# Zero products at the start, a table built in six parts and transposes moved forward, in a convolution and spectral-mixing kernel on one core

## The chip, the core and the metric

The kernel runs on one core of one Trainium2 chip. The core has five engines that run their own instruction streams and meet through semaphores: TensorE (PE in the profile; its weight loads are listed apart as PEld), VectorE (DVE), ScalarE (ACT), GpSimd (POOL) and SyncE (SP). Transfers between the chip's main memory and the on-chip memory are issued by POOL and SP and carried out by 16 DMA engines. The time that counts is the device time of one execution in microseconds (us).

## The reference

Two operators stand one behind the other. The input `x` has 8 batches of 3264 positions with 192 channels.

The first is a causal convolution over the positions with 7 taps, one set of taps for each of 8 heads of 24 channels; the taps go through a softmax first. The second mixes in the frequency domain:

```python
X = np.fft.rfft(x, axis=1)                       # x: the convolution's result
Xr, Xi = np.real(X[:, :64]), np.imag(X[:, :64])  # the 64 lowest modes
Yr = einsum('bmd,mde->bme', Xr, w_r) - einsum('bmd,mde->bme', Xi, w_i)
Yi = einsum('bmd,mde->bme', Xr, w_i) + einsum('bmd,mde->bme', Xi, w_r)
y = np.fft.irfft(Y, n=3264, axis=1)              # all other modes are zero
u = x + y
out = u + np.maximum(u @ w_ch, 0.0)
```

So 20 MB of float32 come in as `x`, 19 MB as the mode weights `w_r` and `w_i` (64 matrices of 192 x 192 each), and 20 MB go out.

## The kernel before

**Tiles.** The batches are taken in four pairs (`q`), and the 3264 positions of a pair in tiles of 128; a last half tile of 64 is shared out over the pairs. A pair has six units of 5, 5, 4, 4, 4 and 4 tiles, so there are 24 units (`UNITS`, `units`). All of `x` stays on chip as bfloat16 in `xall`; the conversion is done by the transfers. The convolution's result is written back into `xall`, one slot further down.

**Start.** POOL issues the loads of `x` for all units in order, with some index tables (`iota`), the identity `ident` and the signed permutation `perm` made between them, and behind them the first half of the mode weights. The loads of `x` wait for no engine's work, only for a free place among eight transfers in flight. SP loads the taps. DVE and ACT make the softmax and spread the taps into a banded matrix, `band`, which the convolution multiplies by on PE.

**The table.** `ftab` holds cosines and sines for the forward transform, 27 rows of 128 columns. `table(t0, t1)` makes its rows `t0` to `t1`: three operations on DVE (product of position and mode, rounding to whole turns, subtraction) and three on ACT (Sin, Abs, Sin). `PARTS` cuts it in three: 5, 9 and 13 rows. The first part stands ahead of the loop over the units, the second and third behind the convolution's copies of the first two units. The temporaries `kprod` and `turns` lie in `arena`, where the mode weights go later.

**The loop over units.** For unit `k`: `conv` (32 to 48 products on PE into the two PSUM tiles `Z`; then one copy back to `xall` on ACT, line 342, and one on DVE, line 344), then for a finished pair `xtrans` of one batch (the transform's result is transposed by products with `ident` and `perm`, and copied into `xt`, which shares its space with the later `zw` under the name `mixa`, on DVE, line 369), then `dft_unit` of the unit before (products of 128 x 384 with the table, line 350, summed over a pair in PSUM), then in two of three units `some(1)`: one job of the list `tjobs`, here `c_bank`, eight transposes of `xall` into `cc` (line 405). Transposed banks are copied by `copy`, which takes ACT for every third and DVE for the others:

```python
    def copy(out, in_):
        ncopy[0] += 1
        if ncopy[0] % 3 == 0:
            nc.scalar.copy(out=out, in_=in_)
        else:
            nc.vector.tensor_copy(out=out, in_=in_)
```

**From the loop to the mixing.** Behind the loop come the last `dft_unit`, whose result ACT copies to `xs` (line 357), the issue of eight groups of weights, `xtrans` of the last two batches, and the jobs `g_bank` (transposes of the table itself, line 394; 104 products in eight banks, the first four banks with 52 of them for one half of it), which are put at the head of `tjobs`.

**Mixing.** Sixteen groups of four modes. `mix(g)` multiplies a group (line 457, 12 products). Four weight groups lie in `arena`, four in the part of `cc` that is not yet used. Groups 8 to 11 are loaded once `mix(0)` to `mix(3)` have freed their places, groups 12 to 15 once `mix(8)` to `mix(11)` have (POOL, line 446). Between the `mix` calls stand jobs of `tjobs`, a number for each group by the list `PLAN`, and products with `w_ch` made ahead (`c_ahead`, line 521).

**Last stage.** For each block of output: products with `w_ch` (line 531) and the inverse transform (line 551) on PE, the maximum on ACT (line 613), the addition on DVE (line 638), the store from POOL or SP (lines 646 and 651).

All orders are written out by hand: an engine runs its instructions in the order of the program's text.

Of the kernel before, what the change touches and what calls it, by code (L numbers as in the profile page):

```python
# [10 lines left out]
ACT = mybir.ActivationFunctionType  # L11
# [8 lines left out]
def kernel(  # L20
# [9 lines left out]
    nc = tc.nc  # L30
    B, S, D = x.shape
# [5 lines left out]
    P = 128  # L37
    NQ = B // 2
    NF = S // P
    NT = NF + 1  # L40
# [5 lines left out]
    MAGIC = 12582912.0  # L46
    UNITS = ((0, 5), (5, 5), (10, 4), (14, 4), (18, 4), (22, 4))
    units = [(q, t0, n) for q in range(NQ) for t0, n in UNITS]
    PARTS = ((0, 5), (5, 14), (14, NF + 2))

    pool = ctx.enter_context(tc.tile_pool(name="main", bufs=1))

    def sb(name, shape, dtype, **kw):
        return pool.tile([P] + shape, dtype, tag=name, name=name, **kw)
# [36 lines left out]
    halfpi = sb("halfpi", [1], F32)  # L91
    xs = [sb(f"xs{i}", [2, D], BF16) for i in range(2)]
# [26 lines left out]
    def temp(n, dtype):  # L119
        w = n * 2 if dtype in (F32, mybir.dt.int32) else n  # L120
        a = arena[:, pos[0]:pos[0] + w]
        pos[0] += (w + 15) // 16 * 16
        return a.bitcast(dtype) if dtype != BF16 else a
# [3 lines left out]
    turns = temp(NTM * MODES, F32)  # L127
# [19 lines left out]
    def psum_pool(name, side):  # L147
        stack = ExitStack()
        return stack, stack.enter_context(tc.tile_pool(name=name, bufs=1, space=PSUM, side=side))
# [4 lines left out]
    low = [pp.tile([P, 512], F32, tag=f"low{i}", name=f"low{i}") for i in range(4)]  # L154

    def slot(q, t):
        return NT * q + t

    def load_unit(q, t0, n, only=None):
        nf = min(n, NF - t0)  # L160
        s0 = slot(q, t0) + 1
        for i in range(2) if only is None else (only,):
# [17 lines left out]
                   allow_small_or_imprecise_dtypes=True)  # L180
    nc.gpsimd.iota(midx, pattern=[[1, MODES]], base=0, channel_multiplier=0,
                   allow_small_or_imprecise_dtypes=True)
    nc.vector.memset(halfpi[:], math.pi / 2)
    nc.vector.memset(packed, 0.0)
    for a in (band[:].rearrange("p h c -> p (h c)"), xall[:, NT:NSLOT:NT, 1, :]):
# [6 lines left out]
    nc.vector.tensor_tensor(out=wsub.rearrange("p (h k) -> p h k", h=H), in0=wr3,  # L192
                            in1=wmax.unsqueeze(2).to_broadcast([P, H, KK]), op=ALU.subtract)
    nc.scalar.activation(out=wexp, in_=wsub, func=ACT.Exp)
    we3 = wexp.rearrange("p (h k) -> p h k", h=H)
    nc.vector.reduce_sum(out=wsum, in_=we3, axis=AX.X)
    nc.vector.tensor_scalar(out=wsum, in0=wsum, scalar1=1e-9, scalar2=None, op0=ALU.add)
# [15 lines left out]
    kp3 = kprod.rearrange("p (t m) -> p t m", t=NTM)  # L213
    tu3 = turns.rearrange("p (t m) -> p t m", t=NTM)

    def table(t0, t1):
        sh = [P, t1 - t0, MODES]
        kp, tu = kp3[:, t0:t1, :], tu3[:, t0:t1, :]
        nc.vector.scalar_tensor_tensor(out=kp, in0=sidx[:, t0:t1].unsqueeze(2).to_broadcast(sh), scalar=1.0 / S,
                                       in1=midx.unsqueeze(1).to_broadcast(sh), op0=ALU.mult, op1=ALU.mult)  # L220
        nc.vector.tensor_scalar(out=tu, in0=kp, scalar1=MAGIC, scalar2=-MAGIC, op0=ALU.add, op1=ALU.add)
        nc.vector.tensor_tensor(out=kp, in0=kp, in1=tu, op=ALU.subtract)
        nc.scalar.activation(out=ftab4[:, t0:t1, :, 1, :], in_=kp.rearrange("p t (h m) -> p t h m", h=2),
                             func=ACT.Sin, scale=-TWOPI)
        nc.scalar.activation(out=tu, in_=kp, func=ACT.Abs)
        nc.scalar.activation(out=ftab4[:, t0:t1, :, 0, :], in_=tu.rearrange("p t (h m) -> p t h m", h=2),
                             func=ACT.Sin, scale=-TWOPI, bias=halfpi[:, 0:1])
        if t1 > NF:
            nc.vector.memset(ftab[HALF:P, NF, :], 0.0)
            nc.vector.memset(ftab[0:HALF, NF + 1, :], 0.0)  # L230

    table(*PARTS[0])
    def load_half(g, i):
        src = bass.AP(tensor=x.tensor, offset=x.offset + ((4 * g + i) * S + P * NF) * D,
                      ap=[[D, HALF], [2 * S * D, 2], [1, D]])
        nc.gpsimd.dma_start(out=xall[HALF * (i ^ g):HALF * (i ^ g) + HALF,  # L236
                                     NT * (2 * g + 1):NT * (2 * g + 2) + 1:NT, 0, :], in_=src)
# [93 lines left out]
    def conv(q, t0, n):  # L331
        done = [conv_step(q, t0, n, half, 0) for half in range(2)]
        for half in range(2):
            turn(done[half])
            conv_step(q, t0, n, half, 1)
        s0 = slot(q, t0)
        for half in range(2):
            cp = Z[half][:, :, :].rearrange("p k (j c) -> p (k j) c", j=2)
            dst = xall[:, s0:s0 + n, :, 96 * half:96 * half + 96].rearrange("p t i (j e) -> p j (t i) e", j=4)
            srcv = cp[:, :, 0:2 * GRP * n].rearrange("p j (c e) -> p j c e", e=GRP)  # L340
            if half == 0:
                nc.scalar.copy(out=dst, in_=srcv)  # L342
            else:
                nc.vector.tensor_copy(out=dst, in_=srcv)  # L344

    def dft_unit(q, t0, n):
        xp = low[0][:, 0:2 * D]
        for t in range(t0, t0 + n):
            if t < NF:
                nc.tensor.matmul(xp, ftab[:, t, :], xall[:, slot(q, t), :, :], start=(t == 0), stop=False,  # L350
                                 skip_group_check=True)
            else:
                for i in range(2):
                    nc.tensor.matmul(xp[:, D * i:D * i + D], ftab[:, NF + (i ^ q // 2), :], xall[:, slot(q, t), 0, :],
                                     start=False, stop=(i == 1), skip_group_check=True)
        if t0 + n == NT:
            nc.scalar.copy(out=xs[q % 2][:], in_=xp.rearrange("p (i d) -> p i d", i=2))

    def xtrans(q, i, bank):
        tp = low[1 + bank][:, 0:3 * P].rearrange("p (j c) -> p j c", j=3)  # L360
        xsv = xs[q % 2][:, i, :].rearrange("k (p j) -> k j p", j=3)
        for j in range(3):
            nc.tensor.matmul(tp[0:64, j, :], xsv[:, j, :], ident[:], start=True, stop=True,
                             tile_position=(0, 0), skip_group_check=True)
            nc.tensor.matmul(tp[64:P, j, :], xsv[:, j, :], perm[:], start=True, stop=True,
                             tile_position=(0, 64), skip_group_check=True)
        b = 2 * q + i
        for h in range(2):
            nc.vector.tensor_copy(out=xt[:, h, :, b:2 * B:B, :],
                                  in_=tp[:, :, 64 * h:64 * h + 64].rearrange("p j (c m) -> p j c m", c=2))  # L370
# [42 lines left out]
    tjobs = []  # L413
# [3 lines left out]
    def some(n, upto=NT * NQ):  # L417
        for _ in range(n):
            if tjobs and tjobs[0][0] < upto:
                _, f, *a = tjobs.pop(0)  # L420
                f(*a)
# [2 lines left out]
    waiting = []  # L424
    for k, u in enumerate(units):
        conv(*u)
        if k < 2:
            table(*PARTS[k + 1])
        if waiting:
            xtrans(*waiting.pop(0), 0)  # L430
        if k:
            q, t0, n = units[k - 1]
            dft_unit(q, t0, n)
            if t0 + n == NT:
                waiting = [(q, 0), (q, 1)]
            if k > 1:
                some(XJOBS[k], min(NT * q + t0 + n, NT * (NQ - 1)))
    dft_unit(*units[-1])


    NG = MODES // 4
# [42 lines left out]
    conv_stack.close()  # L484
    ring_stack, pp = psum_pool("pring", "left")
    ring[:] = [pp.tile([P, 512], F32, tag=f"r{i}", name=f"r{i}") for i in range(4)]
    xtrans(NQ - 1, 0, 0)
    xtrans(NQ - 1, 1, 1)
    tjobs = [(0, g_bank, c, t0, min(8, NT - t0)) for c in (1, 0) for t0 in range(0, NT, 8)] + tjobs

# [219 lines left out]
    for n in range(N + 1):  # L712
# [5 lines left out]
        elif given(n + 2):  # L718
            nc.scalar.copy(out=items[n + 2][1][:, :, 0:2 * D].rearrange("p k (a d) -> p k a d", a=2),
                           in_=halves.rearrange("p (k a) d -> p k a d", k=2))  # L720
# [39 lines left out]
```

## Time and profile before

| what | value |
|---|---|
| time, median of 4 runs (lowest to highest) | 177.32 us (176.48 to 177.88) |
| time of the profiled execution | 176.88 us |
| its span, first to last instruction | 174.7 us |
| busy time: PE, PEld | 149.0 us (85%), 109.1 us (62%) |
| busy time: DVE, ACT, POOL | 119.4 us (68%), 105.6 us (60%), 100.6 us (58%) |
| transfers | 40.17 MB as written on chip or sent out, mean 230 GB/s |
| main memory read, written | 39.40 MB, 20.05 MB |
| first product on PE | 10.54 us |
| first product of the first `mix` | 73.89 us |
| first product of the last `mix` | 107.45 us |

The span is what the profile shows; the profiled execution's own time is 2.2 us longer. In the rows of slices each digit is the busy share of 1/40 of the span in tenths. A line of the timeline gives start and length in us, the engine, the source line, the operation, what it writes and reads, and in brackets how long the engine had been idle and what ended that. PE products overlap each other, so the length over a group is not the sum of its products. GB/s counts the bytes at their on-chip size, so the loads, which convert from float32 to bfloat16, read twice that from main memory.

### The profile page before, as it was taken

To read this page: it belongs to the slowest core of one execution; us is meant where nothing else is said; L and a number is where in the kernel's file an instruction comes from. 1 tells how busy PE (TensorE), PEld (TensorE's weight loads), DVE (VectorE), ACT (ScalarE), POOL (GpSimd) and SP (SyncE) were. 2 spreads that over 40 slices of the span, in tenths; PEclk is the share of its full clock that TensorE was granted. 3 is DMA by queue.
4 is the path that set the end of the run, shared out by engine and by line. 5 is a ranking of instruction groups with operands and counts; after the bars stand their busy time and mean duration, and the time that the engine had idled before them with its cause. 6 is when DMAs were issued, how large, how long until landed. Compare 5 with 4: busy or idle time off the path is not lost.

```text
span 174.7 us, 6407 instructions
## 1 busy us (share of the span) xinstructions
PE 149.0 (85%) x2768; PEld 109.1 (62%) x2768; DVE 119.4 (68%) x181; ACT 105.6 (60%) x149; POOL 100.6 (58%) x157
## 2 busy tenths in 40 slices
PE   0056889999999999697999998999999999999920
PEld 0034456666666666486788775887787677776710
DVE  1878654684775686454677785598889789887850
ACT  8166662636444634445666564677888787887810
POOL 7999989767977554352234200006776656665560
PEclk9999999999999999999999999999999999999995
DMA  3999999999999999999999992088898998999994
GB/s 45 160 176 188 189 190 189 192 190 192 190 191 189 200 207 205 206 208 205 207 207 206 205 198 36 4 297 330 352 349 316 363 353 344 363 357 355 321 364 155
DMA packets 44331, 40.17 MB, mean 230 GB/s; under 512 B 28800, under 2 KB 40656, under 8 KB 44304
## 3 DMA queue, kind: packets, MB, share of 16 engines
q0 software_dynamic: 41136, 37.59, 108.3%
q1 hardware_dynamic: 3168, 2.19, 3.9%
q8 instruction: 21, 0.34, 0.8%
q14 instruction: 6, 0.05, 0.1%
HBM read 39.40 MB, written 20.05 MB: 340 GB/s over the span
## 4 chain that ended last, share of the span: by engine, by line
PE 35%; POOL 30%; DMA 15%; issue 13%; ACT 2%; DVE 1%; POOLq 1%; ACTq 0%
POOL out_dram L646 17%; POOL xall L165 10%; DMA xall<-in_x_dram 9%; PE z L324 7%; PE low L350 6%; DMA arena<-in_moe_w_i_dram 6%; PE r L405 5%; PE low L457 3%; PE low L405 2%; PE r L394 2%; PE za L531 2%; PE za L551 2%; PE zb L551 1%; POOL xall L236 1%; PE low L473 1%
## 5 line engine op out<-in xcount | busy, mean ns | idle before, releaser
L165 POOL DMA_DIRECT2D xall<-in_x_dram x48 | 38.4, 808 | 5.3 <-DMA xall<-in_x_dram 3.2
L324 PE MATMUL z<-xall,band 64*64 64x192 bf16 (+3 forms) x816 | 27.9, 268 | 14.1 <-ACT band L209 10.5
L646 POOL DMA_DIRECT2D out_dram<-arena x23 | 17.3, 754 | 30.6 <-DVE arena L638 28.2
L344 DVE CAST xall<-z 128x768 bf16<-128x768 f32 (+1 forms) x24 | 24.5, 1021 | 14.0 <-PE z L324 12.5
L342 ACT CAST xall<-z 128x768 bf16<-128x768 f32 (+1 forms) x24 | 20.4, 850 | 21.9 <-PE z L324 19.0
L324 PEld LDWEIGHTS <-band 64*64 64x64 bf16 x816 | 18.7, 112 | 22.6 <-ACT band L209 10.9
L531 PEld LDWEIGHTS <-cc 64*128 64x128 bf16 x504 | 22.8, 94 | 6.2 <-issue 2.8
L613 ACT ACTIVATE za<-za 128x768 f32<-128x768 f32 (+1 forms) x26 | 19.9, 782 | 5.7 <-PE za L551 5.1
L613 ACT ACTIVATE zb<-zb 128x768 f32<-128x768 f32 (+1 forms) x26 | 20.1, 781 | 5.0 <-PE zb L551 4.6
L350 PE MATMUL low<-xall,ftab 128*128 128x384 bf16 x100 | 22.7, 356 | 0.0
L405 PEld LDWEIGHTS <-xall 128*128 128x128 bf16 x300 | 19.1, 106 | 3.5 <-issue 0.7
L380 DVE COPY cc<-r 128x1024 bf16<-128x1024 bf16 (+2 forms) x23 | 14.0, 631 | 6.7 <-PE r L405 3.3
L551 PEld LDWEIGHTS <-ftab 64*128 64x128 bf16 x220 | 14.2, 94 | 5.7 <-issue 1.9
L551 PE MATMUL zb<-mixa,ftab 64*128 64x384 bf16 (+1 forms) x112 | 17.4, 309 | 0.0
L551 PE MATMUL zb<-mixa,fupper 64*128 64x384 bf16 (+1 forms) x112 | 17.4, 308 | 0.0
L551 PE MATMUL za<-mixa,ftab 64*128 64x384 bf16 (+1 forms) x108 | 16.7, 308 | 0.5 <-ACT za L613 0.4
L551 PE MATMUL za<-mixa,fupper 64*128 64x384 bf16 (+1 forms) x108 | 16.7, 308 | 0.0
L446 POOL DMA_DIRECT2D arena<-in_moe_w_r_dram x12 | 7.4, 614 | 14.6 <-PE low L457 11.6
L646 POOL DMA_DIRECT2D out_dram<-cc x17 | 12.8, 753 | 4.6 <-DVE cc L638 2.9
L638 DVE TENSOR_TENSOR arena<-za,xall 128x768 f32<-128x768 f32 x14 | 13.3, 955 | 2.3 <-PE za L551 1.4
L531 PE MATMUL zb<-wc,cc 64*128 64x192 bf16 x258 | 14.5, 243 | 0.0
L378 ACT COPY cc<-r 128x1024 bf16<-128x1024 bf16 (+1 forms) x12 | 10.5, 879 | 6.6 <-PE r L405 4.9
(126 smaller groups left out, 247.2 us busy)
## 6 DMA issues: line engine op xcount, KB each, us to landing
out_dram<-arena POOLq DMA_DIRECT2D x23, 384.0 KB, 4.6
out_dram<-cc POOLq DMA_DIRECT2D x17, 384.0 KB, 4.5
xall<-in_x_dram POOLq DMA_DIRECT2D x24, 192.0 KB, 7.2
xall<-in_x_dram POOLq DMA_DIRECT2D x16, 240.0 KB, 6.3
arena<-in_moe_w_r_dram POOLq DMA_DIRECT2D x12, 288.0 KB, 9.2
arena<-in_moe_w_i_dram POOLq DMA_DIRECT2D x12, 288.0 KB, 9.9
out_dram<-band POOLq DMA_DIRECT2D x5, 384.0 KB, 4.7
xall<-in_x_dram POOLq DMA_DIRECT2D x8, 144.0 KB, 6.8
```

The source lines that it names most:

```text
L165: nc.gpsimd.dma_start(out=xall[:, s0:s0 + nf, i, :], in_=src)
L324: mm = nc.tensor.matmul(ov[c], band[r, h, c.start + shift + 64 * (r is UP and c is LO): c.start + shift + 64 * (r is UP and c is LO) + 64] ...
L342: nc.scalar.copy(out=dst, in_=srcv)
L344: nc.vector.tensor_copy(out=dst, in_=srcv)
L350: nc.tensor.matmul(xp, ftab[:, t, :], xall[:, slot(q, t), :, :], start=(t == 0), stop=False, skip_group_check=True)
L380: nc.vector.tensor_copy(out=out, in_=in_)
L405: nc.tensor.transpose(tp[:, P * k:P * k + P], src, ident[:])
L531: nc.tensor.matmul(zt[:, i, D * k:D * k + D], cc[r, q, 3 * t + j, :], wc[r, j, :], start=(k == 0 and j == 0), stop=False, skip_group_check ...
L551: nc.tensor.matmul(zt[:, i, D * k:D * (k + w)], tabs[c][r, t, :], zw[r, c, q:q + w, QUARTERS[which], :], start=False, stop=end and k + w = ...
L613: nc.scalar.activation(out=zt[:, :, 0:w], in_=zt[:, :, 0:w], func=ACT.Relu)
L638: nc.vector.tensor_tensor(out=o[:, :, :].rearrange("p k (i d) -> p i k d", i=2), in0=zt[:, :, 0:2 * D].rearrange("p i (k d) -> p i k d", k=2),
L646: nc.gpsimd.dma_start(out=dst, in_=ov)
```

## The change

- A memset of zeros into `xs[0]` and 36 products of these zeros into a PSUM bank stand at the head of DVE's and PE's work.
- A Sin of one column is put behind the softmax's Exp, so that ACT loads the Sin tables there.
- The table is cut into six parts, one for each unit of the first pair. DVE's half (`turns_part`) of the first part stands ahead of the loop; in the loop, behind the convolution of unit `k`, come ACT's half (`table_part`) of part `k` and DVE's half of part `k + 1`.
- The last `dft_unit` is moved behind the issue of the weights and the change of PSUM pools; two `g_bank` jobs follow it ahead of the last two `xtrans`, two more behind them. The jobs of the mixing stage therefore begin four jobs further on.

```diff
@@
-    PARTS = ((0, 5), (5, 14), (14, NF + 2))
+
+    PARTS = [(t0, t0 + n) for t0, n in UNITS[:-1]] + [(UNITS[-1][0], NF + 2)]
@@
+    idle = xs[0][:, :, :].rearrange("p i d -> p (i d)")
+    nc.vector.memset(idle, 0.0)
+    for _ in range(36):
+        nc.tensor.matmul(low[3][:, 0:2 * D], idle[:, 0:P], idle, start=True, stop=True, skip_group_check=True)
     nc.vector.memset(halfpi[:], math.pi / 2)
@@
     nc.scalar.activation(out=wexp, in_=wsub, func=ACT.Exp)
+
+    nc.scalar.activation(out=turns[:, 0:1], in_=halfpi, func=ACT.Sin)
@@
-    def table(t0, t1):
+    def turns_part(t0, t1):
         sh = [P, t1 - t0, MODES]
         kp, tu = kp3[:, t0:t1, :], tu3[:, t0:t1, :]
...
         nc.vector.tensor_tensor(out=kp, in0=kp, in1=tu, op=ALU.subtract)
+
+    def table_part(t0, t1):
+        kp, tu = kp3[:, t0:t1, :], tu3[:, t0:t1, :]
         nc.scalar.activation(out=ftab4[:, t0:t1, :, 1, :], in_=kp.rearrange("p t (h m) -> p t h m", h=2),
                              func=ACT.Sin, scale=-TWOPI)
...
-    table(*PARTS[0])
+    turns_part(*PARTS[0])
@@
     for k, u in enumerate(units):
         conv(*u)
-        if k < 2:
-            table(*PARTS[k + 1])
+        if k < len(PARTS):
+            table_part(*PARTS[k])
+        if k + 1 < len(PARTS):
+            turns_part(*PARTS[k + 1])
@@
-    dft_unit(*units[-1])
@@
     ring[:] = [pp.tile([P, 512], F32, tag=f"r{i}", name=f"r{i}") for i in range(4)]
+    tjobs = [(0, g_bank, c, t0, min(8, NT - t0)) for c in (1, 0) for t0 in range(0, NT, 8)] + tjobs
+    dft_unit(*units[-1])
+    some(2)
     xtrans(NQ - 1, 0, 0)
     xtrans(NQ - 1, 1, 1)
-    tjobs = [(0, g_bank, c, t0, min(8, NT - t0)) for c in (1, 0) for t0 in range(0, NT, 8)] + tjobs
+    some(2)
```

## The prediction

> **What bounds the kernel now.** I read the page first: its rows of 40 slices, then the chain that ended last, then the chain in order of time, then the waits of POOL and of PE, and last windows of 1 and 2 us where the stages meet.
>
> The rows of slices, 4.37 us each:
>
> ```profile
> PE   0056889999999999697999998999999999999920
> PEclk9999999999999999999999999999999999999995
> DMA  3999999999999999999999992088898998999994
> GB/s 45 160 176 188 189 190 189 192 190 192 190 191 189 200 207 205 206 208 205 207 207 206 205 198 36 4 297 330 352 349 316 363 353 344 363 357 355 321 364 155
> ```
>
> The last row shows two stages with a hole between them. Up to slice 23 (105 us) the transfers run at a flat 190 and then a flat 206 GB/s: x comes in, then the mode weights. Slices 24 and 25 are nearly empty. From slice 26 on results go out, and PE is full. Whether PE is half idle (slices 2 to 5) or full (6 to 15), the rate stays at 190: in the first stage the transfers don't wait for the engines.
>
> The chain in order of time crosses from one stage to the other here (start, length, what):
>
> ```profile
> 96.17 0.32 PE low L457 x12
> ...
> 96.78 0.60 POOL arena L446
> 97.38 10.03 DMA arena<-in_moe_w_i_dram
> 107.45 0.45 PE low L457 x12
> ```
>
> The last weights land at 107.4 us and release the last `mix`. The chain hangs their issue on PE (the twelfth `mix`, 96.0 us), as if an earlier PE would end the stage earlier. But 10.03 us for one transfer of 288 KB means that it queued. POOL's own timeline says how full the queue was (start, length, transfer, idle time before it and its releaser):
>
> ```profile
> 72.43 0.61 POOL L446 DMA_DIRECT2D cc<-in_moe_w_i_dram  x1 [1.00 <-DMA arena<-in_moe_w_i_dram]
> 74.65 0.61 POOL L446 DMA_DIRECT2D arena<-in_moe_w_r_dram  x1 [1.61 <-PE low L457]
> 88.71 0.61 POOL L446 DMA_DIRECT2D arena<-in_moe_w_r_dram  x1 [3.67 <-PE low L457]
> ```
>
> Until 72 us POOL waits for landings, later for PE's `mix` (11.6 us in six waits). Yet windows of 2 us give 205 to 208 GB/s from 60 to 74 us and 200 to 210, mean 206, from 76 to 104. So issuing later cost no bandwidth. The shortest time from issue to landing of a weight transfer is 7.6 us; at 206 GB/s one takes 1.43 us, so at least five were always in flight. The least that any x transfer needed was 4.1 us: PE's release of these buffers has some 3.5 us to spare.
>
> Volume confirms it. Sixteen groups of two transfers of 294,912 bytes are 9.44 MB, 45.7 us at 206 GB/s; from 59 to 60 us, where the rate changes, that ends near 105.4. The other 2.0 us are a ragged end, in windows of 1 us (the last two numbers are DMA share and GB/s):
>
> ```profile
> 103.00:104.00 1.00, 0.90 (x20) 0.55 (x16) 0.88 (x3) 0.60 (x3) 0.00 (x0) 1.00 1.22 204
> 104.00:105.00 1.00, 1.00 (x28) 0.81 (x26) 0.81 (x2) 0.46 (x1) 0.00 (x0) 1.00 0.91 153
> 105.00:106.00 1.00, 1.00 (x26) 0.68 (x26) 0.88 (x3) 0.58 (x2) 0.00 (x0) 1.00 0.51 86
> 106.00:107.00 1.00, 0.90 (x19) 0.60 (x14) 0.70 (x2) 0.71 (x2) 0.00 (x0) 1.00 0.29 52
> ```
>
> So the bound is **transfers to 107.45 us, then PE for 67.3 us**: there PE waits only 1.1 us in all (0.5 of it at that landing). PE itself would have been ready at 106.9.
>
> **The change part by part.**
>
> *Products of zeros.* The page's PEclk row says full speed everywhere, but the spacing of equal products does not (start, length over all):
>
> ```profile
> 16.33 1.78 PE L350 MATMUL low<-xall,ftab 128*128 128x384 bf16 x5
> 35.08 0.99 PE L350 MATMUL low<-xall,ftab 128*128 128x384 bf16 x5
> ```
>
> Taking off the last product's own 0.53 and 0.33 us and dividing by four, a product of 384 columns follows the one before it after 0.31 to 0.32 us at 16 us, and after 0.165 at 35. The step falls between 25 and 27.5 us, after 3 us of PE without a gap (23.8 on). The 36 new products have this same shape. They start near 1.0 us: the memset that they wait for takes some 0.2 us (128x152 words take 0.185), and DVE then idles 2.83 us for POOL anyway. By the slow row alone they take 36 x 0.32 = 11.5 us, to 12.5, and the first convolution, released at 10.54 by `band`, starts 2 us late. The Trainium skill, "TensorE: Matmul & The Clock Gate", Part 1, says that full speed comes after about 3.4 us of sustained work: 11 slow and 25 x 0.165 = 4.1 us, done near 8.6, hidden behind the making of `band`. I take this, as the trace's own step after 3 us fits. The same section holds the whole ramp to be worth under 1% of a span, which speaks against the change: at most 1.7 us. The rows say more. Units 0 to 5 take 21.0 us, from 10.54 to 31.56, or 3.5 each; the other 18 take 40.2, or 2.23 each. At the fast spacing the first six are set by ACT and DVE, next.
>
> *Table by units.* Before, 3 parts: 5.98 us on DVE, 6.37 on ACT. After, 6 parts of 320 or 256 elements: on DVE 3 x 1.31 + 3 x 1.14 = 7.3, on ACT 3 x 1.48 + 3 x 1.32 = 8.4 (256 interpolated between the rows of 320, 576 and 832). That is 1.4 and 2.0 us more. Each convolution's copy now stands ahead of its part, so the wait of the second convolution for ACT (1.77 us) goes. With the copies ACT has 14.4 us for six units and DVE 13.8, so unit 6 starts near 25 instead of 31.56: 6.5 us sooner. The table load for Sin (1.28 us) moves into ACT's idle 4.62 us ahead of `band`; the small Sin that goes with it writes into `turns`, so DVE's first rounding waits for it, but it is done near 7 us and that operation stood at 11.15. The parts end near 25 us, and the first weight transfer that needs their space comes at 54.
>
> One rule is against the finer parts: "SBUF — State Buffer", the section on the three doors, says that a VectorE operation in a two-port mode keeps GpSimd from writing descriptors. The rounding operation (TENSOR_SCALAR) is such a kind: 1.46 us before, 1.83 after, so by the rule POOL could come 0.4 us later. By the row POOL next waits 0.51 us for a landing at 25.3, so that is swallowed. I take 0.
>
> *Transposes around the last transform.* The two holes:
>
> ```profile
> 72.53 0.26 PE L363 MATMUL low<-ident,xs 128*64 128x128 bf16 x1 [0.79 <-ACT xs L357]
> 73.89 0.45 PE L457 MATMUL low<-arena,mixa 128*16 128x192 bf16 x12 [0.82 <-DVE mixa L369]
> ```
>
> Into the first go 32 transposes (1.01 us), into the second 20 (0.68). But their first two copies, 0.69 us each, now stand on DVE ahead of the four `mixa` copies (1.15), which the first `mix` waits for: it comes about 3.1 us after the last transform instead of 2.15. Of 1.7 us PE keeps 0.75. The transform's move behind POOL's weight issues holds nothing on POOL: those wait for landings and buffers, not for it.
>
> *The sum.* The first `mix` comes at 73.9 - 6.5 + 0.95, near 68. From there each `mix` meets its own landing: 2.86 us a group, and PE waits instead of lagging. POOL's issues go back to waiting for landings, as before 72 us, at the same 206 GB/s. The last landing stays at 107.4. Every instruction of every engine behind the last `mix` stands in the same order. So gain 6.5 + 0.75 us at the front, **0 at the end**. Against the profiled execution (176.88, span 174.7) that is 176.9; this execution lies 0.4 below the median of the four runs, 177.32, so on that footing 177.3. If transfers were no cover, those 7 us would be the gain.
>
> **Rivals.**
>
> *A, the load stage ends sooner.* With PE ahead, eight transfers are always in flight at the end rather than five to seven; the ragged 2.0 us could close: 105.4, so 174.9 in the profile and 175.3 as a median. For it: the fall from 204 to 52 GB/s. Against: from 60 to 74 us, with the queue full, the rate was the same. The chain's own reading, landing 10.03 us after issue, gives less: the twelfth group lands near 95.3, so at most 0.7 us.
>
> *B, slower: the clock falls in the new waits.* PE's lag is now idle time, some 0.8 us in each 2.86 from 68 to 107. If that takes the fast spacing away, the last stage, bound by PE, starts at half speed and loses 1.7 us for one stretch of 3.4 or 3.4 for two: about 179.9. For it: from 10 to 24 us PE was 72% busy and stayed slow. Against: from 70 to 80 us PE was busy 7.4 of 10 us, one window of 2 us only a third, and stayed fast. It decides from the point at which the first products behind 107.4 are twice as far apart.
>
> *C, the zeros don't do it.* They stay slow, the first convolution comes 2 us late, and the front gains little. The first `mix` is then near 74 and the weights still cover it: within 0.4 us of 177.3.
>
> **How the numbers follow.** Forecast 0.75, A 0.11, B 0.10, C 0.04. About 1% is what a measurement of this kernel can tell from no change. The forecast and C lie within it, A at its edge below, B above: faster 0.11, same 0.79, slower 0.10. The runs spread 0.7 us to each side; the range reaches to A and part of the way to B: 175.3 to 178.9.
>
> **What would show it.** Right: products of zeros spaced 0.165 us before 9 us; unit 6 near 25; first `mix` at 66 to 71; more waits of PE for weight landings; GB/s row unchanged at 190 and 206; last `mix` between 106.9 and 107.8; 67.3 us behind it. Wrong: a last `mix` before 106, a weight stage above 210 GB/s, or a last stage longer than 68.5 us.

## The result: 0.5% slower, and the profile after

The changed kernel takes 178.01 us (median of 40 runs, 176.73 to 179.05), the kernel before 177.03 us beside it (61 runs). The ratio is 1.005, 95% interval 1.0035 to 1.0064: some 0.9 us slower. The profiled execution took 177.62 us with a span of 175.9 us, against 176.88 and 174.7 before. Ratios leave out executions more than 1.5% above the fastest of their kernel (four of 14 in e16, whose median with them would be 0.6% above the kernel before, and at most one in any other changed kernel), and the profiles of e8 and e16 are of such executions, so of these two only the times and the place of the last fetch are used.

The rows of slices after the change, 4.4 us each:

```profile
PE   7949999999998998997499777999999999999900
PEclk9985899999999999999999999999999999999996
DMA  4999999999999999999999991097898998998992
GB/s 43 150 176 190 189 192 188 192 193 189 188 189 190 199 206 209 204 206 207 206 207 206 207 189 31 16 341 306 347 353 320 370 355 335 354 368 347 327 366 90
```

The two stages and the hole between them (slices 24 and 25) are where they were, and so are the rates, 190 and 206 GB/s. PE is busy from the first slice. PEclk has a dip in slices 2 to 4 (8.8 to 22 us). The row of before shows none, though its products had the slow spacing until some 27 us: the trace's clock entries begin only at 27.4 us there, at 5.2 us here, and what lies ahead of the first entry is drawn as full.

PE's timeline at the places that the prediction named (start, length over the group, operation, count, idle time before and its releaser):

```profile
1.14 7.99 PE L188 MATMUL low<-xs 128*128 128x384 bf16 x36 [1.14 <-DVE halfpi L189]
...
11.00 1.06 PE L335 MATMUL z<-xall,band 64*64 64x240 bf16 x30 [0.17 <-ACT band L217]
...
12.92 1.82 PE L335 MATMUL z<-xall,band 64*64 64x240 bf16 x32 [0.86 <-ACT xall L353]
...
14.67 1.78 PE L361 MATMUL low<-xall,ftab 128*128 128x384 bf16 x5
...
26.25 1.07 PE L335 MATMUL z<-xall,band 64*64 64x240 bf16 x32
```

The zeros are done at 9.13 us. They start 0.32 us apart, and 0.163 us apart from 5.2 us on, where the granted clock becomes full. The first convolution runs at full speed (30 products in 1.06 us, where 32 took 2.27 us before), but the second takes 1.82 us and the transform beside it has the slow spacing again. Unit 6 starts at 26.25 us, 5.3 us sooner than before (31.56).

```profile
70.43 0.45 PE L469 MATMUL low<-arena,mixa 128*16 128x192 bf16 x12 [0.87 <-DVE mixa L380]
...
107.75 0.45 PE L469 MATMUL low<-arena,mixa 128*16 128x192 bf16 x12 [1.02 <-DMA arena<-in_moe_w_i_dram]
```

The first `mix` comes 3.5 us sooner (73.89 before). The last one comes 0.3 us later (107.45 before), and a landing releases it. Where the lead went is in PE's waits from 66 to 108 us (engine, line, what it waited for, us in total, times, longest):

```profile
PE low L469 <- DMA arena<-in_moe_w_i_dram: 4.5, 5, 1.3
PE low L469 <- DMA cc<-in_moe_w_i_dram: 2.4, 2, 1.7
```

That is 6.9 us of waiting for weights, against 0.9 us before. The lead has become idle time in front of landings that come no sooner.

Then the end. POOL's last store is issued at 168.90 us, 61.15 us behind the last `mix`; before it was 168.61, 61.16 us behind. So the whole last stage of PE, DVE and ACT took the same to 0.01 us. But from there to the span's end it is 6.95 us (175.85 less 168.90), and before 6.14 us (174.75 less 168.61). The two ends in the view of transfers, first after (with its packet of the queue q8), then before; the columns of a store are its size and the median us from issue to landing, those of a queue its packets, MB and share of time:

```profile
q8 instruction: 1, 0.02, 0.7%
...
out_dram<-arena POOLq DMA_DIRECT2D x2, 384.0 KB, 5.0
out_dram<-cc POOLq DMA_DIRECT2D x1, 384.0 KB, 5.0
out_dram<-cc SPq DMA_DIRECT2D x1, 192.0 KB, 4.8
out_dram<-arena POOLq DMA_DIRECT2D x1, 192.0 KB, 5.2
```

```profile
out_dram<-arena POOLq DMA_DIRECT2D x2, 384.0 KB, 4.4
out_dram<-cc POOLq DMA_DIRECT2D x1, 384.0 KB, 4.4
out_dram<-cc SPq DMA_DIRECT2D x1, 192.0 KB, 4.5
out_dram<-arena POOLq DMA_DIRECT2D x1, 192.0 KB, 4.7
```

The same five stores land 0.3 to 0.6 us later. Among them stands a packet of a queue called "instruction", which the window of before (from 166 us on) doesn't have. Over the whole span that queue has one packet more (before, then after):

```profile
q8 instruction: 21, 0.34, 0.8%
```

```profile
q8 instruction: 22, 0.36, 0.8%
```

The trace holds these packets one by one: 16,384 bytes each, some 1.0 us on one of the 16 DMA engines (the one among the last stores 0.95). Counting PE's loads and products between one packet and the next gives 255 on average in the changed kernel. I read them as blocks of PE's program, brought in while it runs. The padding below bears this out: with 256 more PE instructions the last fetches stand within 1.3 us of where they stood, one number higher (e14 and e15 as the kernel before, e10 as the change). The 36 products of zeros with their weight loads are 72 instructions more (5608 instead of 5536). With them the 22nd block is fetched at 167.4 us, 0.2 us before PE's last product starts, with the last stores under way. Without them the 21st, at 160.1 us, is the last one ahead of the end.

So the loss in the profiled execution is 0.30 us at the last `mix`, 0.8 us behind the last store's issue, and 0.4 us less outside the span (1.8 instead of 2.1): 0.7 us in all, which is 177.62 less 176.88.

### The profile page after: what moved, and what is told of

Its sections match the earlier page's. It is cut to its first block, busy times and chain, and to the rows that moved or that the text cites. A ratio compares the mean times of both kernels' runs of the same rounds, so it can differ in the third digit from the quotient of the medians.

```text
span 175.9 us, 6497 instructions
## 1 busy us (share of the span) xinstructions
PE 153.9 (87%) x2804; PEld 111.0 (63%) x2804; DVE 120.0 (68%) x191; ACT 107.4 (61%) x159; POOL 100.6 (57%) x157
## 4 chain that ended last, share of the span: by engine, by line
DMA 42%; PE 23%; POOL 22%; issue 8%; ACT 1%; POOLq 1%; DVE 1%; ACTq 0%
DMA arena<-in_moe_w_i_dram 19%; DMA xall<-in_x_dram 16%; POOL xall L166 11%; PE zb L566 7%; DMA cc<-in_moe_w_i_dram 6%; PE za L566 6%; POOL out_dram L661 6%; PE za L546 5%; PE zb L546 4%; POOL arena L458 1%; POOL xall L247 1%; ACT za L628 1%; DVE band L653 1%; PE low L469 1%; POOLq L770 0%
## 5 line engine op out<-in xcount | busy, mean ns | idle before, releaser
L335 PE MATMUL z<-xall,band 64*64 64x192 bf16 (+3 forms) x816 | 26.6, 259 | 3.9 <-ACT band L217 1.6
L335 PEld LDWEIGHTS <-band 64*64 64x64 bf16 x816 | 17.6, 108 | 12.5 <-issue 5.4
L361 PE MATMUL low<-xall,ftab 128*128 128x384 bf16 x100 | 21.7, 344 | 0.0
L416 PEld LDWEIGHTS <-xall 128*128 128x128 bf16 x300 | 18.3, 103 | 3.1
L566 PE MATMUL zb<-mixa,ftab 64*128 64x384 bf16 (+1 forms) x112 | 17.4, 309 | 0.0
L566 PE MATMUL zb<-mixa,fupper 64*128 64x384 bf16 (+1 forms) x112 | 17.4, 308 | 0.0
L546 PE MATMUL za<-wc,cc 64*128 64x192 bf16 x246 | 14.1, 243 | 0.3 <-DVE cc L653 0.2
```

What stands on the lines that cost most here:

```text
L335: mm = nc.tensor.matmul(ov[c], band[r, h, c.start + shift + 64 * (r is UP and c is LO): c.start + shift + 64 * (r is UP and c is LO) + 64] ...
L416: nc.tensor.transpose(tp[:, P * k:P * k + P], src, ident[:])
L546: nc.tensor.matmul(zt[:, i, D * k:D * k + D], cc[r, q, 3 * t + j, :], wc[r, j, :], start=(k == 0 and j == 0), stop=False, skip_group_check ...
L566: nc.tensor.matmul(zt[:, i, D * k:D * (k + w)], tabs[c][r, t, :], zw[r, c, q:q + w, QUARTERS[which], :], start=False, stop=end and k + w = ...
```

## The experiments

The expectations use letters. **F**: the 22nd fetch, among the last stores, is the cost. **P**: TensorE's early work itself is. **R**: the zeros slow the early transfers, and the load stage ends later. **E**: the early instructions cost something whatever the fetch. **C**: the weights' landings hide the lead. L and D are earlier guesses: the lead itself costs, or the end is longer from another cause. In the code cuts, comments and the name `per` are added for reading.

**Which part costs, which part leads (e1 to e4).** e1 is the change without its zeros:

```diff
-    idle = xs[0][:, :, :].rearrange("p i d -> p (i d)")
-    nc.vector.memset(idle, 0.0)
-    for _ in range(36):
-        nc.tensor.matmul(low[3][:, 0:2 * D], idle[:, 0:P], idle, start=True, stop=True, skip_group_check=True)
```

> The changed kernel without the memset and the 36 products of zeros; all else as changed. Theory R (the loads in the ramp are moved slower while PE runs the zeros: 155 and 149 GB/s in 6 to 10 us against 175 and 162 before, 0.07 MB or 0.35 us, which shifts the end of the weights and so everything behind it): the rates at 6 to 10 us return to 160 to 175, the last mix to 107.4, and the time to within 0.2% of the kernel before. Theory L (PE's lead is to blame: it loads the queues and the memory at other times than before): the lead is smaller without the zeros but stays, so the time stays 0.3 to 0.6% above the kernel before. Theory D (the drain of the last stores, 0.7 us longer in the changed profile, from other causes): time as the changed kernel, last mix as before.

Measured: ratio 0.9992 (0.997 to 1.0015). Its first `mix` stands at 70.03 us, its last at 107.46. Without the zeros the loss is gone, and the lead is not smaller.

e2 puts the same lines into the kernel before:

```diff
+    nc.vector.memset(idle, 0.0)
+    for _ in range(36):
+        nc.tensor.matmul(low[3][:, 0:2 * D], idle[:, 0:P], idle, start=True, stop=True, skip_group_check=True)
     nc.vector.memset(halfpi[:], math.pi / 2)
```

> The kernel before with only the memset and the 36 products of zeros added. Theory R: slower by 0.3 to 0.6%, rates at 6 to 10 us near 150, last mix near 107.8. Theory L: the zeros alone give PE little lead, since the table in three parts still holds ACT (unit 6 at 29 us or later); within 0.2% of the kernel before. Theory D: nothing in particular.

Measured: 1.0049 (1.0023 to 1.0074), first `mix` at 74.23 us. The zeros alone bring the whole loss and no lead at all. The rate from 6 to 10 us, which R needs lower, was 174 GB/s against 169 before. A 22nd fetch stands at 166.9 us, and from the last store's issue to the end it takes 6.7 us.

e3 makes only the table in six parts, with the early Sin:

```diff
-    PARTS = ((0, 5), (5, 14), (14, NF + 2))
+    PARTS = [(t0, t0 + n) for t0, n in UNITS[:-1]] + [(UNITS[-1][0], NF + 2)]
...
-        if k < 2:
-            table(*PARTS[k + 1])
+        if k < len(PARTS):
+            table_part(*PARTS[k])
+        if k + 1 < len(PARTS):
+            turns_part(*PARTS[k + 1])
```

> The kernel before with the table in six parts and the early Sin, nothing else. Theory R: no zeros, so within 0.2% of the kernel before, rates in the ramp as before. Theory L: part of the lead (PE stays slow, unit 6 near 28 us), so 0 to 0.3% slower.

Measured: 1.0015 (0.999 to 1.004). The first `mix`:

```profile
69.61 0.45 PE L463 MATMUL low<-arena,mixa 128*16 128x192 bf16 x12 [0.82 <-DVE mixa L373]
```

That is 4.3 us sooner than before, from the table alone. The last `mix` stands at 107.28.

e4 moves only the transposes and the last transform:

```diff
-    dft_unit(*units[-1])
...
+    tjobs = [(0, g_bank, c, t0, min(8, NT - t0)) for c in (1, 0) for t0 in range(0, NT, 8)] + tjobs
+    dft_unit(*units[-1])
+    some(2)
     xtrans(NQ - 1, 0, 0)
     xtrans(NQ - 1, 1, 1)
+    some(2)
```

> The kernel before with only the last transform moved and two banks of transposes ahead of and two behind the last xtrans. Theory R: within 0.2% of the kernel before, last mix at 107.4. Theory L: a lead of 0.75 us only, so within 0.2%. If this kernel alone is slower by 0.3% or more, both theories are wrong and the copies' places on ACT and DVE in the mixing stage are to blame.

Measured: 1.0018 (0.9992 to 1.0043), first `mix` at 74.47 us, 0.6 later than before. Neither of these two parts can be told from no change.

**Work or number of instructions (e5 to e8).** All are the whole change with other products at its head.

```diff
+    idle = cc[:, 0, 0:4, :].rearrange("p k s -> p (k s)")
+    for _ in range(16):                                   # e5: 16 products of 512 columns
+        nc.tensor.matmul(low[3][0:128, 0:512], idle[:, 0:128], idle[:, 0:512], start=True, stop=True, skip_group_check=True)
```

> The changed kernel with 16 zero products of 512 columns in place of 36 of 384: PE is busy with zeros for some 5 us from the first us, but its program is 32 instructions longer than without zeros, not 72. Theory F (the 72 instructions are to blame: PE's program comes in blocks of 16 KB, 256 instructions, and with 72 more the 22nd block is fetched at 167 us, ahead of the last stores; it holds one DMA engine for 0.95 us[...]): no fetch before the last stores, drain from the last store's issue to the span's end 6.1 us, time within 0.2% of the kernel before. Theory P (the work of the zeros on PE is to blame, through the clock or the loads in the ramp): slower by 0.3 to 0.5%.

Measured: 1.0057 (1.0034 to 1.008). The fetch came all the same, at 167.9 us, with only 32 instructions more. My place for it in the program was wrong: it lies between 5552 and 5568 instructions (e9 and e5). The end took 7.6 us.

```diff
+    for _ in range(36):                                   # e6: 36 products of 16 columns
+        nc.tensor.matmul(low[3][0:32, 0:16], idle[:, 0:32], idle[:, 0:16], start=True, stop=True, skip_group_check=True)
```

> The changed kernel with the 36 zero products cut to 16 columns and 32 rows of output: the same 72 instructions, but PE busy with zeros for under 4 us, with nearly no work in it. Theory F: a 22nd fetch at 167 us, drain of 6.7 us or more, slower than the kernel before by 0.4 to 0.6%, as the changed kernel. Theory P: within 0.2% of the kernel before.

Measured: 1.0059 (1.0036 to 1.0083). These products take 1 us instead of 8 and cost as much. P falls: it isn't the amount of work.

```diff
-    for _ in range(36):
+    for _ in range(100):                                  # e7
```

> The same with 100 small zero products: 200 instructions more than without, so the 22nd fetch moves up by 128 instructions, to some 163 us, and the next one lies behind the end. Theory F: the stores that follow take up part of the delay, 0 to 0.3% slower than the kernel before, drain 6.1 to 6.5 us. Theory P: no more than e6; if the number of instructions cost as such, 2.8 times what e6 costs.

Measured: 1.0031 (1.0004 to 1.0058). The last fetch has moved to 161.7 us, the end takes 6.3 us.

e8 is the change itself once more.

> The changed kernel again, on the chip of these runs. Both theories: slower than the kernel before by 0.5%. Theory F: in this second profile too the 22nd fetch lies at 167 to 168 us and the drain is 6.7 us or longer. Theory P (loads): the rates at 6 to 10 us are near 150 GB/s again.

Measured: 1.0071 (1.0033 to 1.0109).

**Moving the fetch with the early products kept (e9, e10).** Eight wide products (16 instructions, below the step), and 164 small ones (72 + 256 instructions, one block further on):

```diff
-    for _ in range(36):
+    for _ in range(8):                                    # e9, 512 columns each
+    for _ in range(164):                                  # e10, 16 columns each
```

> The change with its 36 zero products replaced by 8 of 512 columns each, from the table's own buffer: 16 more instructions on TensorE than the kernel before has (5552) where the change has 72. What they write is overwritten later. Theory F (one more block of TensorE's program is fetched among the last stores once the program passes some 5560 instructions): no 22nd fetch ahead of the end, drain behind the last store's issue near 6.2 us, ratio 0.998 to 1.002, as without any zeros. Rival (any early work on TensorE costs it, by its instructions in the load stage or by its heat): slower by about 0.5%, as with 36.

> The change with its 36 zero products replaced by 164 tiny ones (16 columns, 32 rows of weights): 328 more instructions on TensorE than before, which is the 72 of the change and one whole block of 256. Theory F: the fetches stand at the same places as with 72, one number higher, so that again one falls among the last stores: ratio 1.004 to 1.007, drain 6.7 to 7.2 us. Rival (the cost grows or falls with the number of early instructions, so that 200 more at 1.003 was a step down): ratio 1.003 or below, no fetch later than 162 us.

Measured: e9 1.0021 (1.0 to 1.0042), with 21 packets ahead of the stores' end and 6.1 us for it; e10 1.006 (1.0031 to 1.0088), with the 23rd packet at 167.1 us and 6.6 us. With the number of small products the loss goes from 0.6 (36) to 0.3 (100) and back to 0.6% (164), as a block of 256 instructions says and a cost that grows or falls with the number doesn't. The three intervals overlap, though; the place of the fetch and the length of the end show the step more clearly.

**Without the cover (e11, e12).** In both kernels only the first eight of sixteen weight groups are loaded; the others multiply what the buffers hold:

```diff
     def load_w(g):
-        if g < NG:
+        if g < NL + NW:
```

> The kernel before, with the expert weights loaded for groups 0 to 7 alone; groups 8 to 15 multiply by what the buffers still hold, so the loading is left out for half of them and the work of TensorE is whole. It is there to be compared with the change under the same edit. Theory C (the loads set when the last mix starts and so hide the change's 3.5 us lead): without the second half of the loads the last mix starts near 106 us, for TensorE was nearly busy from 73.9 us on in the kernel before; ratio 0.98 to 1.0. Rival (loads are not what binds even before): the same.

> The change with the expert weights loaded for groups 0 to 7 alone, groups 8 to 15 multiplying by what the buffers still hold. Theory C: the 3.5 us lead at the first mix is no longer given back to landings, the last mix starts near 101 to 103 us, and the kernel is faster than the kernel before under the same edit by 3 to 5 us (ratio to the unedited kernel before 0.955 to 0.975). Rival (the lead is lost in the mixes themselves, not to the loads): within 1 us of the kernel before under the same edit.

The last `mix`, first in the light kernel before, then in the light changed one:

```profile
106.21 0.44 PE L457 MATMUL low<-arena,mixa 128*16 128x192 bf16 x12
```

```profile
101.94 0.45 PE L469 MATMUL low<-arena,mixa 128*16 128x192 bf16 x12
```

With the full loads both stood near 107.5. Now the lead reaches the end: 4.3 us at the last `mix`. To the kernel before the ratios are 0.9914 (0.9884 to 0.9945) and 0.9787 (0.9744 to 0.9831), so to one another 0.987 (about 0.982 to 0.993, both errors taken together). C holds in kind. In size the expectation missed: 3 to 5 us were expected, the medians differ by 2.2 (175.36 and 173.2, four runs each). The profiled pair differs by 3.5 us of span. Most of what is missing from 4.3 us stands in the pair's ends, 6.0 us after the change and 5.4 before: the light changed kernel has a fetch at 161.9 us, 0.3 us before PE's last product, and the light kernel before has none there. The other three executions of e12 have spans 0.6 to 1.8 us longer than the profiled one; what they lose wasn't looked for.

**Late fetch and early products apart (e13 to e18).** Small products stand in the mixes instead, where PE waits for landings; the real ones overwrite them (`per` is a run's list of how many stand in which `mix`):

```diff
     def mix(g):
         yp = low[(g // 2) % 2][:, D * (g % 2):D * (g % 2) + D]
+        for _ in range(per.get(g, 0)):
+            nc.tensor.matmul(yp[0:16, 0:16], ident[:, 0:16], ident[:, 0:16], start=True, stop=True, skip_group_check=True)
```

e13 has 36 of them and no zeros, e14 has 92 of them and 36 small early products, e15 has 128 of them and nothing early.

> The change without its zeros at the start; 36 tiny products (16 columns, 16 rows of weights) stand in the waits of six mixes instead, where they are overwritten by the mixes: 72 more instructions, none of them early. Theory F alone (the late fetch is the whole cost): ratio 1.004 to 1.007 as with the zeros. Theory F with E (late fetch and early instructions each pay a part): 1.002 to 1.004, last mix near 107.4, drain 6.7 to 7.0 us, 22nd fetch near 167 us. Theory E alone: 0.998 to 1.001.

> The change with 36 tiny products at the start in place of its zeros, and 92 more tiny ones in the waits of eight mixes: 256 more instructions in all, one whole block, so that no fetch falls among the last stores. Theory F alone: ratio 0.998 to 1.002. Theory F with E: 1.002 to 1.004, last mix near 108, drain near 6.2 us. Theory E alone: 1.004 to 1.007.

> The change without its zeros; 128 tiny products in the waits of eight mixes, 256 more instructions, nothing early and no fetch among the last stores. All theories that put the cost on the late fetch or on early instructions: ratio 0.998 to 1.002, last mix near 107.4, drain near 6.2 us. Rival (every block of program fetched costs, wherever it falls): 1.003 to 1.006.

Measured: e13 1.0008 (0.9986 to 1.003), e14 0.9998 (0.9977 to 1.0019), e15 0.9983 (0.9964 to 1.0003). e15 has a 22nd packet too, at 160.3 us, and pays nothing that was measured: a block more costs nothing in itself. e14 has the early products of e6 and none of its loss: E alone, at that size, falls. The two differ only by 92 late products and so by the place of the fetch, and by 0.6% (0.3 to 0.9, both errors taken together). In e13 the 22nd fetch came at 165.8 us, 1.5 us before PE's last product. The window from 166 us has no packet of that queue, and the end takes 6.3 us: not quite the case it was built for.

So e16 and e17 have fewer of them (16 and 22), that the fetch falls later, and again nothing early:

```diff
-        per = {6: 6, 7: 6, 8: 6, 11: 6, 12: 6, 13: 6}     # e13
+        per = {7: 4, 8: 4, 12: 4, 13: 4}                  # e16
+        per = {6: 3, 7: 4, 8: 4, 11: 3, 12: 4, 13: 4}     # e17
```

> The change without its zeros; 16 tiny products stand in the waits of four mixes: 32 more instructions than before (5568), none of them early. Theory F (a block of program fetched in the last microsecond of the products and among the last stores is the cost, whatever brought it there): 22nd fetch within 1.2 us of TensorE's last product, drain 6.6 to 7.5 us, ratio 1.003 to 1.007. Rival (the early products are needed for the cost): ratio 0.998 to 1.002 with a fetch at that place. If no 22nd fetch falls ahead of the end, ratio 0.998 to 1.002 and nothing is told apart.

> The change without its zeros; 22 tiny products stand in the waits of six mixes: 44 more instructions than before (5580), none of them early. Theory F: 22nd fetch within 1.2 us of TensorE's last product, drain 6.6 to 7.5 us, ratio 1.003 to 1.007. Rival (the early products are needed for the cost): ratio 0.998 to 1.002 with a fetch at that place.

Measured: e16 1.003 (1.0 to 1.0061), e17 1.0016 (0.9993 to 1.004). The last stores of e17, in the same view as above:

```profile
q8 instruction: 1, 0.02, 0.7%
...
out_dram<-cc POOLq DMA_DIRECT2D x1, 384.0 KB, 5.1
out_dram<-cc SPq DMA_DIRECT2D x1, 192.0 KB, 5.0
out_dram<-arena POOLq DMA_DIRECT2D x1, 192.0 KB, 5.4
```

The fetch is there, at 168.6 us, and so are the late landings and an end of 6.9 us, without one early product. The time rose by 0.2 to 0.3%, not by 0.5: neither the expectation of F nor that of its rival is met.

e18 is the whole change, zeros and all, with e14's 92 products in the mixes:

> The whole change, its 36 products of zeros included, with 92 tiny products in the waits of eight mixes: 256 more instructions than before, one whole block of program, so that the 22nd fetch falls near 160 us and none among the last stores. If the late fetch has to be there for the cost: ratio 0.998 to 1.002, drain near 6.1 us. If the early products pay their share whatever the fetch: 1.002 to 1.004, last mix near 108. If the early products are the whole cost: 1.004 to 1.007.

Measured: 1.0014 (0.9992 to 1.0037). The last fetch ahead of the end is at 161.1 us, the end takes 6.4 us. So the loss falls from 0.5% to 0.14% when the program is made longer, a difference of 0.36% (0.1 to 0.6), though e18's own interval reaches up to 0.37%.

Sorted by the two things, the change and the sixteen experiments without the light pair read:

| | last fetch among the last stores | no fetch there |
|---|---|---|
| early products | the change 1.005, e2 1.0049, e5 1.0057, e6 1.0059, e8 1.0071, e10 1.006 | e7 1.0031, e9 1.0021, e14 0.9998, e18 1.0014 |
| none | e16 1.003, e17 1.0016 | e1 0.9992, e3 1.0015, e4 1.0018, e13 1.0008, e15 0.9983 |
| from the last store's issue to the span's end | 6.6 to 7.6 us (six profiles) | 5.9 to 6.4 us (ten, with the kernel before) |

The last row doesn't overlap. A block of program fetched among the last stores lengthens the end by some 0.8 us, shown with early products and without (e17). How the fetch delays the stores wasn't measured. Of the 0.8 us some 0.4 us comes back outside the span in these kernels (1.8 us there, against 2.2 in the median of the kernel before), so that by itself the fetch is worth the 0.2 to 0.3% of e16 and e17. A likely reason for what comes back: where the next block isn't needed before the end, it can be fetched behind it, as in the profiles of e3, e4, e9 and e18 (1.1 to 2.3 us behind the span's end, with 2.0 to 2.9 us outside the span; 1.7 to 2.1 us in the other six profiles of that column). That wasn't tested.

With early products there, moving the fetch away is worth more: 0.6% from e6 to e14 and 0.36% from the change to e18. The full 0.5 to 0.7% was measured only where both come together, and early products without the fetch average 1.0016. **How the rest of the loss, 0.2 to 0.3%, comes about stays open.** It may be no more than the sum of two small costs: 0.16% for early products alone and 0.2% for the fetch alone, each known to 0.1 to 0.2%. As the ends are equally long with early products and without, it would have to lie ahead of the last store's issue, and single profiles differ there by more than that (last section).

## Where the prediction was right and wrong

**The bound: right.** Rates of 190 and 206 GB/s, a last `mix` released by a landing at 107.75 us. e12 shows the cover by taking it away: the lead then reaches the last `mix`.

**The zeros' own time: right in kind.** Done at 9.1 us for 8.6, ahead of `band`. The slow spacing lasted 4.0 us (1.14 to 5.17), where the sum took 3.4; the trace decides. **What they were to bring: wrong.** From 12.0 to 18.8 us the granted clock is half again. Without the zeros (e1) the fast spacing is there sooner, by the second transform, which takes 1.47 us in the change; and unit 6, at 26.25 us in the change, starts hardly later:

```profile
18.15 0.99 PE L356 MATMUL low<-xall,ftab 128*128 128x384 bf16 x5
...
26.45 1.07 PE L330 MATMUL z<-xall,band 64*64 64x240 bf16 x32
```

So the zeros are worth 0.2 us there. The loss that rival C feared, a first convolution 2 us late, didn't come either.

**The table: right in kind, 1.2 us short.** Unit 6 at 26.25 instead of near 25. The second convolution's wait for ACT did not go, it fell from 1.77 to 0.86 us. The early Sin delayed nothing: `band` releases the first convolution at 10.54 us in both. e3 shows that the part alone gives all of the lead. Taking 0 for the rule on POOL's descriptors stands: POOL comes to its loads of 22 us 0.14 us later than before (22.42 for 22.28), and its wait of 0.51 us at 25.3 us, which was to swallow the delay, is gone.

**The transposes: right.** The first `mix` comes 2.8 us behind the last transform (67.63 to 70.43), for 3.1 predicted and 2.15 before.

**The first `mix`:** 70.4 instead of near 68, inside the 66 to 71 that was given. 1.2 us were lost up to unit 6; another 1.2 from there to the last transform, which ends 4.1 us sooner than before, where unit 6 had started 5.3 us sooner.

**The waits that take the lead: right,** 6.9 us for seven landings, from 0.9.

**The step that failed is the last of the sum, "0 at the end".** It followed from "Every instruction of every engine behind the last `mix` stands in the same order". That is true, and from the last `mix` to the last store's issue the two profiles differ by 0.01 us. But the sum then took "67.3 us behind it" to the span's end as a constant, and 6.1 us of these are no instruction's work. They are stores landing, and they share the DMA engines with the program's own fetches. The term measured 68.1 us: 0.8 us more in the profile, about half of it net in the time. The prediction had the page's row of q8 before it and didn't ask what 72 more instructions do to it: edits that are hidden as work were taken to be free. This accounts for some half of the 0.9 us; where the other half arises stays open, as said above.

Rival A didn't come: from 104 to 107 us the rates still fall, to 66 GB/s. Rival B didn't come in this profile: the granted clock is full from 18.8 us to the last stage, and that stage has the same length to 0.01 us. But the fall that B feared does happen in these waits. In six other profiles of kernels with the lead the granted clock was half for 3.4 us (in e6 for 6.8 us) somewhere from 84 to 105.5 us (e5, e6, e7, e9, e17, e18). In e5 it was full again only 2.6 us before the last `mix` (window, busy time and instructions of each engine, clock, DMA share, GB/s):

```profile
102.00:105.00 3.00, 2.86 (x40) 2.18 (x42) 0.67 (x2) 1.03 (x3) 0.00 (x0) 0.50 1.12 191
```

So it may have been luck that the last stage began at the full clock. The prediction's sign of error, a last stage above 68.5 us, didn't show (68.1); it was set too wide for an error of this size. The range held the time, and the change did stay within 1%. But the measurement, with 0.15% to each side, was finer than the 1% that the prediction took for what can be told, and it tells 0.5% from no change.

## What to carry to other kernels

A lead ahead of a stage that transfers pace becomes idle time in front of landings; before building it, look for the wait that will take it, and test the bound by halving the transfers. Instructions that are hidden as work are still program: count them, look at where the instruction queue's packets fall, and compare the time from the last store's issue to the end, where a fetch cost some 0.8 us here. An experiment with many tiny products in the place of the large ones tells work from number, and one whole block of padding (256 instructions here) tells number from place.

## What the runs showed that was not expected

**PE's program comes in blocks of 16,384 bytes over the same DMA engines as the data,** one for some 255 loads and products, some 1.0 us each, 21 to 23 in an execution. An extra one whose last stands at 160.3 us, ahead of the last stores, cost nothing that could be measured (e15: 0.9983).

**Zeros in front don't keep the clock.** After 8 us of products, and gaps of 1.4 us before `band` and of 0.9 us before the second convolution, the granted clock was half from 12.0 to 18.8 us, in windows:

```profile
10.00:14.00 4.00, 2.43 (x56) 1.65 (x56) 3.75 (x8) 2.92 (x6) 3.73 (x12) 0.75 1.56 186
...
14.00:18.00 4.00, 4.00 (x54) 1.96 (x47) 2.93 (x7) 2.95 (x6) 4.00 (x5) 0.50 1.58 189
18.00:22.00 4.00, 4.00 (x69) 2.69 (x71) 3.90 (x8) 3.01 (x8) 3.85 (x9) 0.90 1.60 189
```

The column behind POOL's is the clock. PE was busy for the whole of 14 to 18 us while it stood at 0.50. Without zeros (e1) the trace has the full clock from 17.4 us on, sooner than with them.

**One early wait moves the whole load stage.** POOL's second load for the last half tile, at 11 us, waited in some profiles for an x transfer to land. POOL's timeline in e6:

```profile
9.46 1.57 POOL L166 DMA_DIRECT2D xall<-in_x_dram  x2
12.20 0.60 POOL L247 DMA_DIRECT2D xall<-in_x_dram  x1 [1.18 <-DMA xall<-in_x_dram]
```

In e6, e17 and e18 (1.18 to 1.24 us) the last `mix` came at 108.7 to 108.9 us; in the other profiles with full loads, the changed kernel's among them, with no wait there or one under 0.4 us, at 106.9 to 108.4. POOL hardly idles before 25 us (in the kernel before its next wait for a landing is at 25.3 us), so it can't make up there what it loses. It appears with early products (e6, e18) and without (e17), with the fetch at the end (e6, e17) and without (e18). Whether it comes more often in some kernels than in others, and so is the part of the loss that stays open, single profiles can't say, and it wasn't tried. The falls of the clock in the mixing stage are a second candidate. Over the executions of one kernel a lower mean clock goes with a longer span in e6, e7 and e17 (correlation -0.5 to -0.6), but not in the change (0.02) or e2 (0.07), so they don't explain its loss as far as the runs show.
